# Gated linear attention and a GELU network: last output chunk by column halves, odd positions' sums by subtraction, another order

## The chip, the cores and the metric

The kernel runs on one core of a Trainium2 chip. The time is the device time of one execution in microseconds (us); of the kernel before there are 14 executions, with a median of 183.11 us (182.71 to 183.54). The core has a matrix engine (TensorE, PE in the profile, with its weight loads as PEld), VectorE (DVE), ScalarE (ACT) and GpSimd (POOL), and SyncE (SP), which issues most transfers. Matmul results lie in eight banks of PSUM.

## The reference

Attention with a decaying state, per batch (4) and head (8), over 768 positions with 48 numbers each:

```python
f = 1.0 / (1.0 + np.exp(-f_logit))
for t in range(S):
    state = f[:, :, t, :, None] * state + np.einsum('bhd,bhe->bhde', k[:, :, t], v[:, :, t])
    y[:, :, t] = np.einsum('bhd,bhde->bhe', q[:, :, t], state)
```

The result, as 3072 tokens of 384 numbers, goes through a network with 2048 hidden numbers:

```python
h = x @ w_in
g = 0.5 * h * (1.0 + erf(h * inv_sqrt2))
out = g @ w_out
```

## The kernel before

**Attention by chunks.** The 3072 tokens are 24 chunks of 128, six to a batch. Two chunks make a unit (12 units). Within a chunk the recurrence is made of products: with G the running sum of log f over the chunk, keys are scaled by exp(-G) and queries by exp(G); the masked scores of scaled queries and keys times v give the part from within the chunk; the scaled queries times the state before the chunk give the rest; and the state goes on by the keys times v and by the decay over the whole chunk. A batch's last chunk (5, 11, 17, 23) hands no state on.

**Units 0 to 4 are loaded in pairs** (`PAIRS`): each partition holds two neighbouring positions of a head, an even and an odd one, so that a transfer's pieces are twice as long. Rows 0 to 63 are then the unit's first chunk and rows 64 to 127 its second. The other units hold a chunk in their 128 rows.

**Steps and names.** An operation's name is a letter code with the number of its unit or chunk.

- `decays` (from L452): E and L (L479, L482) make -log f of a whole unit on ScalarE, in `lf`. C (L495 to L505) are TensorE's running sums, by multiplication with triangular matrices: in a pair unit two 128x384 matmuls for the even positions (C of the even number) and two for the odd ones, and eight narrow matmuls with `negp` (L505) for the decay over each of the two chunks; in other units one 128x384 matmul and four one-column ones with `negcol` (L497) per chunk. RG and GT (L510, L512) are exp(-G) and exp(G), GL (L515, L519) the decay over the chunk, all on ScalarE. KP and QP (L525) are the scaled keys and queries in `sc`, mostly on VectorE; VC (L530) casts v on GpSimd.
- `turn`: T (L558) transposes keys and queries on TensorE for units 0 to 3, KQ copies the result out; from unit 4 on a transposing transfer, KD (L546), does it.
- `attn_pair` and `attn_nat`: A are the scores (L724, L662), masked by VectorE (AM, L571); S the state product (L746, L685), `carry` its sum on VectorE (R, L591 and L595), decay (T, L597) and cast (SB, L602) on GpSimd; YI (L766) with YX (L645), or Y (L639, L698), the output, YB (L615) its copy. In a pair unit the matmuls use 64-row or 64-column tiles of the array; these operations have `mode=1`.
- X: the output is transposed for the network, by TensorE (L631) for units 0 to 4 and by a transposing transfer XD (L619) afterwards.
- `ffn_group`, one group per unit: eight F1 products (L802, six 128x256 matmuls each, hidden numbers by tokens), each followed by a GELU on ScalarE (GE, L812), then per chunk four F2 products (L821, four 128x384 matmuls each), added up in one bank; O (L836) copies the result, st (L841) stores it. For the last chunk, 23, the two halves of the columns are copied by ScalarE and VectorE (L829) and stored by two queues (L831).

**Banks.** `BANKS = (4, 0, 4)`: banks 0 to 3 (`s_fh`) are for F1 and F2 products and, at the start, for a few others; banks 4 to 7 (`s_m`) for the attention. An F1 product gives its bank back when its GELU has read it.

**Order.** The kernel issues nothing as it is written: `P.add` lists operations with an engine, an assumed duration, what they read and write, the buffers they use, and a priority; `Plan.run` places them one by one on its own clock, by the time at which they could start and then by priority, and so fixes each engine's order (each engine works through its order strictly). Priorities get a random part per range of 20 in the priority's number (`SEEDS`). ScalarE needs one table for exp and log and another for GELU; the planner groups these uses, and 15 loads (L870) stand between them, besides the first. `LOADS` is the order of the first loads: f, k, v, q of a unit (f2 is that of unit 2; u all four), i and o pieces of the two weight matrices, issued by GpSimd. In `load`, a transfer that follows one of the other queue is held until an earlier transfer of that queue has landed; for a load on SP this is the last but one of them.

**Filler.** At the end of the listing, before an operation that opens a bank and is planned before 30 us, matmuls of zeros are put in, as many as the planned idle time of TensorE holds (L864). They write the bank that the operation then uses.

Of the kernel before, what the change touches and what calls it, by code (L numbers as in the profile page):

```python
# [12 lines left out]
ALU = mybir.AluOpType  # L13
# [13 lines left out]

SEEDS = [0, 684, 383, 3363, 2427, 131, 74, 3619, 3555, 1021, 519, 3174]

# [52 lines left out]
class Plan:  # L82
# [30 lines left out]
    def run(self):  # L113
# [4 lines left out]
        for o in self.ops:  # L118
            if o.prio > -5:
                k = min(max(int(o.prio % 1000) // 20, 0), len(SEEDS) - 1)  # L120
                o.prio += rng.uniform(-SPREAD, SPREAD)
                if SEEDS[k]:
                    w = (0.5, 1.0, 3.0, 8.0)[SEEDS[k] % 4]
                    o.prio += own[k].uniform(-w, w)
        act, switched, mode = None, 0.0, 0
        port = {"DVE": (0.0, 0.0), "POOL": (0.0, 0.0)}
# [77 lines left out]


SIZES = [2, 2, 2, 2, 2, 2, 2, 2, 2, 2, 2, 2]
PAIRS = [0, 1, 2, 3, 4]
# [15 lines left out]
AJ = [2, 3, 4, 5, 6, 7, 8, 10, 11]  # L223
NGT = 4
ROWS = [16, 17, 18, 19]
WARM = 30.0
LOADS = ['f0', 'k0', 'v0', 'q0', 'f1', 'v1', 'k1', 'q1', 'i0', 'k2', 'f2', 'v2', 'q2', 'i1', 'i2', 'i3', 'o0', 'o1', 'o3', 'f3', 'o2', 'k3', 'q3', 'u4', 'v3']
LOADS += [f"u{n}" for n in range(12) if f"u{n}" not in LOADS and f"c{2 * n}" not in LOADS and f"f{n}" not in LOADS]
# [3 lines left out]
def kernel(  # L232
# [53 lines left out]
    s_gt, s_rg = slots(3, [C, HD], F32, "gt"), slots(3, [C, HD], F32, "rg")  # L286
    s_gl = slots(6, [C, 2, P2], F32, "gl")
    s_kq = slots(3, [C, 2, P2, 2, C], BF16, "kq")
    s_am = slots(8, [C, P2, C], BF16, "am")
# [52 lines left out]
    for i in range(3):  # L342
        P.add("DVE", 0.2, lambda i=i: nc.vector.memset(
            s_sb.tiles[i].rearrange("p a b -> p (a b)").bitcast(F32), 0.0), wr=[f"sbz{i}"], prio=-70)
    z_lf = [f"lfz{i}" for i in range(3)]
    z_sc = [f"scz{i}" for i in range(NQ)]
# [105 lines left out]
    def decays(u):  # L452
# [16 lines left out]
        for a, b, lo, hi in parts:  # L469
# [7 lines left out]
            def expop(lo=lo, hi=hi):  # L477
# [6 lines left out]
                  bufs=[fl, lf], table="exp", prio=pr, name=f"L{u}")  # L484
        gps = [(s_fh if u in EG else s_m).new() for _ in range(2)]
        for j, n in enumerate(ns):
            y = X[n]
            gt, rg = s_gt.new(), s_rg.new()
            y.update(sc=s_sc.new(), vb=s_vb.new())
            pr = 20 * u + 10 * j  # L490

            def cum(j=j, g=gps[j]):
                g = g.t()
                if not pair:
                    nc.tensor.matmul(g[:, 0:HD], trin, lf.t()[:, j, :, 0:D], start=True, stop=True)  # L495
                    for p in range(P2):
                        nc.tensor.matmul(g[:, HD + p:HD + p + 1], lf.t()[:, j, 2 * p:2 * p + 2, :], negcol,  # L497
                                         start=True, stop=True, skip_group_check=True)
                    return
                nc.tensor.matmul(g[:, 0:HD], trip[:, 0, :], lf.t()[:, 0, :, 0:D], start=True, stop=False)  # L500
                nc.tensor.matmul(g[:, 0:HD], trip[:, 1 - j, :], lf.t()[:, 1, :, 0:D], start=False, stop=True)
                if j:
                    for i in range(2):
                        for p in range(P2):
                            nc.tensor.matmul(g[:, HD + 2 * p:HD + 2 * p + 2], lf.t()[:, i, 2 * p:2 * p + 2, :], negp,  # L505
                                             start=False, stop=(i == 1), skip_group_check=True)
            P.add("PE", (0.54 if j else 0.33) if pair else 0.27, cum,
                  rd=([("lf", u, 0), ("lf", u, 1), "trip", "negp"] if pair else [("lf", u, j), "trin", "negcol"]), wr=[("g", n)],
                  bufs=[lf, gps[j], gt, rg, y["sc"], gl], prio=pr, opens=gps[j], name=f"C{n}")
            P.add("ACT", 0.40, lambda g=gps[j], rg=rg: nc.scalar.activation(rg.t(), g.t()[:, 0:HD], AF.Exp, scale=-1.0),  # L510
                  rd=[("g", n)], wr=[("rg", n)], bufs=[gps[j], rg], table="exp", prio=pr, name=f"RG{n}")
            P.add("ACT", 0.40, lambda g=gps[j], gt=gt: nc.scalar.activation(gt.t(), g.t()[:, 0:HD], AF.Exp),  # L512
                  rd=[("g", n)], wr=[("gt", n)], bufs=[gps[j], gt], table="exp", prio=pr + 1, name=f"GT{n}")
            if not pair:
                P.add("ACT", 0.19, lambda g=gps[j], j=j: nc.scalar.activation(  # L515
                    gl.t()[:, j, :], g.t()[:, HD:HD + P2], AF.Exp),
                    rd=[("g", n)], wr=[("gl", n)], bufs=[gl, gps[j]], table="exp", prio=pr + 2, name=f"GL{n}")
            elif j:
                P.add("ACT", 0.19, lambda g=gps[j]: nc.scalar.activation(  # L519
                    gl.t(), g.t()[:, HD:HD + 2 * P2].rearrange("a (p c) -> a c p", c=2), AF.Exp),  # L520
                    rd=[("g", n)], wr=[("gl", n - 1), ("gl", n)], bufs=[gl, gps[j]], table="exp", prio=pr + 2,
                    name=f"GL{n}")
            for w, nm, a, b, off in ((0, "kp", "kt", rg, 0), (1, "qp", "qt", gt, 1)):
                pl = n in (GKP, GQP)[w]
                P.add("POOL" if pl else "DVE", 0.80 if pl else 0.475, lambda w=w, a=a, b=b, y=y, j=j, pl=pl: (nc.gpsimd if pl else nc.vector).tensor_tensor(  # L525
                    y["sc"].t()[:, w, :, 0:D], half(u, x[a], j), b.t().rearrange("p (h d) -> p h d", h=H), ALU.mult),
                    rd=[("gt" if w else "rg", n), (a, n)] + z_sc, wr=[(nm, n)], bufs=[y["sc"], x[a], b], prio=pr + off,
                    port=True, name=f"{nm.upper()}{n}")
# [39 lines left out]
    def mask_scores(aps, ams, key, nm, rd, pr, mk, mkey):  # L568
        for hh in range(2):
            pl = key[1:] + (hh,) in GAM  # L570
            P.add("POOL" if pl else "DVE", 1.15 if pl else 0.61, lambda hh=hh, pl=pl: (nc.gpsimd if pl else nc.vector).tensor_tensor(  # L571
                ams[hh].t(), aps[hh].t().rearrange("p (h t) -> p h t", t=C),
                mk.unsqueeze(1).to_broadcast([C, P2, C]), ALU.mult),
                rd=[rd, mkey], wr=[key + (hh,)], bufs=[aps[hh], ams[hh]], prio=pr + PRI["A"], name=nm)
# [131 lines left out]
    def attn_pair(u):  # L706
# [52 lines left out]
        def intra():  # L759
            for hh in range(2):  # L760
                for p in range(P2):
                    h = 2 * p + hh
                    for jk in range(2):
                        for cc in range(2):
# [4 lines left out]
                                             skip_group_check=True)  # L769
        P.add("PE", 0.5, intra, mode=1, rd=[("am", u, a, b) for a in range(2) for b in range(2)] + [("vb", n) for n in ns],  # L770
              wr=[("yi", n) for n in ns] + ([("yp", n0)] if osb is None else []), bufs=yps + vbs + sum(ams, []) + [U[u]["yb"]],
              prio=pr + PRI["Y"], opens=yps[0], name=f"YI{u}")
        for cc, n in enumerate(ns):
            o = (osb, mid)[cc]
# [8 lines left out]
    def ffn_group(g):  # L783
# [11 lines left out]
        for u in range(FO // pk):  # L795
# [11 lines left out]
            def gelu(u=u, hps=hps):  # L807
                to, fr = gT.t()[:, u * pk:(u + 1) * pk, :].rearrange("p a b -> p (a b)"), hps.t()
                if U[ns[0] // 2]["pair"]:
# [4 lines left out]
                  name=f"GE{g}.{u}")  # L814
        for s_ in range(s):
            op, osb = s_fh.new(), s_os.new()
            n = first[g] + s_
            for r in range(4):
                def f2(s_=s_, r=r, op=op):
                    for fo in range(4 * r, 4 * r + 4):  # L820
                        nc.tensor.matmul(op.t()[:, 0:d_model], gT.t()[:, fo, s_ * C:(s_ + 1) * C], wout[fo // 4][:, fo % 4, :],  # L821
                                         start=(fo == 0), stop=(fo == FO - 1))
                P.add("PE", 0.65, f2, rd=[("gT", g, fo // pk) for fo in range(4 * r, 4 * r + 4)] + [f"wout{r}"],
                      wr=[("o", n)], bufs=[op, gT], prio=pr + PRI["F"] + s_, held=True, name=f"F2.{n}.{r}")
            if n == NCH - 1:
                osbs = (osb, s_os.new())
                for i, eng in enumerate(("ACT", "DVE")):
                    h = slice(i * d_model // 2, (i + 1) * d_model // 2)
                    P.add(eng, 0.27, lambda h=h, i=i, op=op, osb=osbs[i]: copier(not i)(osb.t()[:, h], op.t()[:, h]),  # L829
                          rd=[("o", n)], wr=[("os", n, i)], bufs=[op, osbs[i]], prio=pr - 1000, name=f"O{n}")  # L830
                    P.add("DMA", 0.3, lambda h=h, i=i, n=n, osb=osbs[i]: (nc.sync if i else nc.scalar).dma_start(  # L831
                        out=out[n * C:(n + 1) * C, h], in_=osb.t()[:, h]), rd=[("os", n, i)], bufs=[osbs[i]], prio=-5, lag=4.0,
                        name=f"st{n}")
                continue
            od = n in ODVE
            P.add("DVE" if od else "ACT", 0.475 if od else 0.40, lambda op=op, osb=osb, od=od: copier(not od)(osb.t(), op.t()[:, 0:d_model]),  # L836
                  rd=[("o", n)], wr=[("os", n)], bufs=[op, osb], prio=pr - 1000, name=f"O{n}")
            def store(n=n, osb=osb):
                w = C // 2 if n in ROWS else C
                for r in range(0, C, w):  # L840
                    nc.sync.dma_start(out=out[n * C + r:n * C + r + w, :], in_=osb.t()[r:r + w, :])  # L841
            P.add("DMA", 0.6, store, rd=[("os", n)], bufs=[osb], prio=-5, lag=4.0, name=f"st{n}")

    g = 0
# [59 lines left out]
```

## Time and profile before

| | |
|---|---|
| median of 14 executions | 183.11 us (182.71 to 183.54) |
| the profiled execution | 183.15 us |
| its span, from first to last instruction | 181.0 us |
| TensorE matmuls busy | 172.6 us (95%), 1991 instructions |
| ScalarE busy | 126.2 us (70%) |
| VectorE busy | 95.6 us (53%) |
| GpSimd busy | 52.5 us (29%) |
| F1 matmuls (L802) | 576, 273 ns each |
| F2 matmuls (L821) | 384, 326 ns each |
| GELU (L812) | 96, 667 ns each |
| table loads (L870) | 15, 1283 ns each |
| TensorE clock granted | full all through |

A row of the profile names line, engine and operation, then what is written and read, with its shape. A matmul's duration there includes the time until its last result is out, which overlaps with the next matmul; what a matmul costs in a dense run is the distance from its start to the next start. Where the order of time is shown, a bracket gives the engine's idle time before the instruction and what ended it. One execution has been profiled.

### The profile page before, as it was taken

Reading aid. Unit: us, or ns where it says so; the run is one execution under the profiler, and the core shown is the slowest. Engines: PE = TensorE matmul, PEld = TensorE weight load, DVE = VectorE, ACT = ScalarE, POOL = GpSimd, SP = SyncE. Lnnn points to the kernel's source line nnn. Section 1 sums busy time; section 2 is a strip of 40 time slices with the busy share of each in tenths; the row PEclk is TensorE's granted clock in tenths of the full one; section 3 lists DMA queues with packets and bytes.
Section 4 is the critical chain, followed back from the end, with each engine's and each line's share of the span. In section 5 each row is a group of like instructions: output and inputs, shape, how many; then the busy total and the mean of one; then the engine's idle time right before and its main releaser. Section 6 shows DMA issues by size and latency. Waiting matters only on the chain.

```text
span 181.0 us, 4913 instructions
## 1 busy us (share of the span) xinstructions
PE 172.6 (95%) x1991; PEld 131.8 (73%) x1991; DVE 95.6 (53%) x185; ACT 126.2 (70%) x215; POOL 52.5 (29%) x116
## 2 busy tenths in 40 slices
PE   7789989999999999999999999999999999999992
PEld 2356669865778977669679689966696976886961
DVE  4289730068898640689277771627785307171020
ACT  2775298992986899988957789687493698360910
POOL 7657870003224801251352014014353111100000
PEclk9999999999999999999999999999999999999999
DMA  5999999999989897999999979989999963812112
GB/s 143 267 261 224 272 187 210 216 259 270 274 154 234 164 213 140 221 187 213 176 201 229 179 153 231 179 172 160 193 249 120 222 118 74 175 48 43 43 43 87
DMA packets 106997, 32.61 MB, mean 180 GB/s; under 512 B 102112, under 2 KB 106080, under 8 KB 106976
## 3 DMA queue, kind: packets, MB, share of 16 engines
q1 hardware_dynamic: 105056, 29.07, 78.2%
q0 software_dynamic: 1776, 3.15, 9.7%
q8 instruction: 15, 0.25, 0.6%
q10 hardware_dynamic: 144, 0.10, 0.2%
q14 instruction: 6, 0.05, 0.1%
HBM read 25.17 MB, written 4.72 MB: 165 GB/s over the span
## 4 chain that ended last, share of the span: by engine, by line
PE 76%; DMA 8%; SPq 6%; ACT 4%; DVE 2%; issue 2%; DVEq 0%; ACTq 0%
PE ps L802 33%; PE ps L821 30%; SPq L434 6%; DMA fl<-in_f_logit_dram 6%; DMA xT<-yb 2%; PE ps L662 2%; PE ps L698 2%; ACT L870 1%; PE ps L495 1%; ACT gT L812 1%; PE ps L639 1%; DVE sc L525 1%; PE ps L685 1%; PE ps L724 1%; PE ps L558 1%
## 5 line engine op out<-in xcount | busy, mean ns | idle before, releaser
L812 ACT ACTIVATE gT<-ps 128x512 bf16<-128x512 f32 x96 | 58.4, 667 | 23.5 <-PE ps L802 21.9
L802 PE MATMUL ps<-xT,win 128*128 128x256 bf16 x576 | 68.6, 273 | 0.2 <-DMA xT<-yb 0.2
L821 PE MATMUL ps<-wout,gT 128*128 128x384 bf16 x384 | 68.3, 326 | 0.0
L802 PEld LDWEIGHTS <-win 128*128 128x128 bf16 x576 | 61.3, 114 | 2.6 <-issue 0.4
L821 PEld LDWEIGHTS <-gT 128*128 128x128 bf16 x384 | 35.9, 98 | 20.9
L525 DVE TENSOR_TENSOR sc<-kt,rg 128x384 bf16<-128x384 f32 x23 | 14.5, 632 | 29.1 <-ACT rg L510 28.2
L597 POOL TENSOR_TENSOR tn<-rr,gl 128x384 f32<-128x384 f32 x16 | 13.9, 868 | 40.8 <-DVE rr L595 35.8
L530 POOL CAST vb<-vt 128x384 bf16<-128x384 f32 x22 | 12.1, 560 | 44.9 <-DMA vt<-in_v_dram 44.8
L571 DVE TENSOR_TENSOR am<-ps,mask 128x512 bf16<-128x512 f32 x28 | 17.5, 684 | 12.3 <-PE ps L662 12.3
L836 DVE COPY osb<-ps 128x384 f32<-128x384 f32 x20 | 11.1, 555 | 23.7 <-PE ps L821 17.6
L870 ACT ACT_TABLE_LOAD x15 | 19.2, 1283 | 0.3
L602 POOL CAST sb<-tn 48x192 bf16<-48x192 f32 x40 | 14.5, 362 | 13.3 <-DVE tn L591 7.7
L615 DVE CAST yb<-ps 128x384 bf16<-128x384 f32 x22 | 12.0, 555 | 7.3 <-PE ps L698 4.1
L510 ACT ACTIVATE rg<-ps 128x384 f32<-128x384 f32 x24 | 12.0, 502 | 5.4 <-PE ps L497 4.6
L512 ACT ACTIVATE gt<-ps 128x384 f32<-128x384 f32 x24 | 11.8, 499 | 5.6 <-PE ps L505 3.7
L479 ACT ACTIVATE fl<-fl 128x768 f32<-128x768 f32 x12 | 10.2, 854 | 6.5 <-DMA fl<-in_f_logit_dram 6.4
L571 DVE TENSOR_TENSOR am<-ps,maskp 128x512 bf16<-128x512 f32 x20 | 12.5, 684 | 2.6 <-PE ps L724 2.5
L525 DVE TENSOR_TENSOR sc<-qt,gt 128x384 bf16<-128x384 f32 x23 | 13.0, 571 | 1.2 <-DMA kt<-in_k_dram 0.9
L864 PE MATMUL ps<-junk 128*128 128x512 bf16 (+2 forms) x35 | 10.1, 421 | 1.9 <-POOL junk L856 1.3
L482 ACT ACTIVATE lf<-fl 128x768 bf16<-128x768 f32 x12 | 10.1, 844 | 0.4
L595 DVE TENSOR_TENSOR rr<-ps,tn 128x384 f32<-128x384 f32 x16 | 8.8, 553 | 1.4 <-POOL tn L597 0.5
L864 PEld LDWEIGHTS <-junk 128*128 128x128 bf16 x35 | 3.5, 111 | 5.9 <-issue 3.2
(68 smaller groups left out, 125.3 us busy)
## 6 DMA issues: line engine op xcount, KB each, us to landing
out_dram<-osb SPq DMA_DIRECT2D x19, 192.0 KB, 2.3
fl<-in_f_logit_dram SPq DMA_DIRECT2D x14, 192.0 KB, 3.8
kt<-in_k_dram SPq DMA_DIRECT2D x14, 192.0 KB, 3.9
qt<-in_q_dram SPq DMA_DIRECT2D x14, 192.0 KB, 3.8
vt<-in_v_dram SPq DMA_DIRECT2D x14, 192.0 KB, 3.7
fl<-in_f_logit_dram SPq DMA_DIRECT2D x5, 384.0 KB, 5.6
kt<-in_k_dram SPq DMA_DIRECT2D x5, 384.0 KB, 5.9
vt<-in_v_dram SPq DMA_DIRECT2D x5, 384.0 KB, 6.7
```

What stands on the lines that cost most here:

```text
L510: P.add("ACT", 0.40, lambda g=gps[j], rg=rg: nc.scalar.activation(rg.t(), g.t()[:, 0:HD], AF.Exp, scale=-1.0), rd=[("g", n)], wr=[("rg", n ...
L525: P.add("POOL" if pl else "DVE", 0.80 if pl else 0.475, lambda w=w, a=a, b=b, y=y, j=j, pl=pl: (nc.gpsimd if pl else nc.vector).tensor_tensor(
L530: P.add("ACT" if hv else "POOL", 0.40 if hv else 0.47, lambda y=y, j=j, hv=hv: (nc.scalar.copy if hv else nc.gpsimd.tensor_copy)(y["vb"].t ...
L571: P.add("POOL" if pl else "DVE", 1.15 if pl else 0.61, lambda hh=hh, pl=pl: (nc.gpsimd if pl else nc.vector).tensor_tensor(ams[hh].t(), ap ...
L597: P.add("POOL", 0.83, lambda: nc.gpsimd.tensor_tensor(tn.t(), rr.t(), glb(), ALU.mult), rd=[("rr", n), ("gl", n)], wr=[("tn", n)], bufs=[r ...
L602: P.add("POOL", 0.36, lambda hh=hh: nc.gpsimd.tensor_copy(sb.t()[64 * hh:64 * hh + D, :, D * hh:D * hh + D], tn.t()[64 * hh:64 * hh + D, : ...
L615: P.add("ACT" if help_ else "DVE", 0.40 if help_ else 0.475, lambda: copier(help_)(yb.t()[:, i, :], yp.t()[:, 0:HD]), rd=[("yp", n)], wr=[ ...
L802: nc.tensor.matmul(hps.t()[:, i * tok:(i + 1) * tok].rearrange("a (s t) -> a s t", s=s), col(fo)[:, kk, :], xT.t()[:, :, kk, :], start=(kk ...
L812: nc.scalar.activation(to, fr, AF.Gelu)
L821: nc.tensor.matmul(op.t()[:, 0:d_model], gT.t()[:, fo, s_ * C:(s_ + 1) * C], wout[fo // 4][:, fo % 4, :], start=(fo == 0), stop=(fo == FO ...
L864: nc.tensor.matmul(o.opens.t()[:, 0:w], junk[:, 0:C], junk[:, 0:w], start=True, stop=True, skip_group_check=True)
L870: nc.scalar.preload_act_table_set({"exp": "natural_log_exp_and_others", "gelu": "gelu_and_others"}[o.table])
```

## The change

- **Column halves.** The second product (F2) of chunk 23 is made in two runs of 16 matmuls of 192 columns, for the first and the second half of the columns, each in a bank of its own. Each half is copied and stored as before, the first by ScalarE and its queue, the second by VectorE and SP.
- **Odd positions.** In units 2, 3 and 4 (`G1D`) the running sum at an odd position is the one at the even position before it less the odd position's own -log f: one VectorE subtraction (G), from PSUM and `lf` into a new SBUF tile, in place of two matmuls. The narrow matmuls for the chunk ends go to the even positions' operation.
- **No unused decay.** For the last chunk of a batch the narrow matmuls and the exponential of the decay are left out (in unit 2, the eight matmuls have one column instead of two). The decay tiles are set to 1 at the start by six memsets on VectorE.
- **Pair outputs.** In units 2, 3 and 4 (`YJ`) YI and YX are one operation.
- **Order.** Other `SEEDS`, and in `LOADS` the piece o2 stands before f3, not behind it. `NUDGE`, `XA`, `GLD` and `AMX` are empty or zero and change nothing.

```diff
-SEEDS = [0, 684, 383, 3363, 2427, 131, 74, 3619, 3555, 1021, 519, 3174]
+SEEDS = [1643, 41, 3215, 1275, 2533, 2502, 823, 887, 1264, 763, 2447, 3095]
...
-LOADS = [..., 'o1', 'o3', 'f3', 'o2', 'k3', 'q3', 'u4', 'v3']
+LOADS = [..., 'o1', 'o3', 'o2', 'f3', 'k3', 'q3', 'u4', 'v3']
...
+    for i in range(6):
+        P.add("DVE", 0.07, lambda i=i: nc.vector.memset(s_gl.tiles[i], 1.0), wr=[f"glz{i}"], prio=-60)
...
+        last = 2 * u + 1 if (2 * u + 1) % nC == nC - 1 else None
+            ends = 1 if last else 2
...
-                    for p in range(P2):
+                    for p in range(0 if gld or n == last else P2):
                         nc.tensor.matmul(g[:, HD + p:HD + p + 1], lf.t()[:, j, 2 * p:2 * p + 2, :], negcol,
...
+            if j and g1d:
+                P.add("DVE", 0.475, lambda a=gps[0], b=gps[1]: nc.vector.tensor_tensor(
+                    b.t().rearrange("p (h d) -> p h d", h=H), a.t()[:, 0:HD].rearrange("p (h d) -> p h d", h=H),
+                    lf.t()[:, 1, :, 0:D], ALU.subtract), ..., name=f"G{n}")
...
+        if u in YJ:
+            olds = [(cc, o) for cc, o in enumerate((osb, mid)) if o is not None]
+            def joint():
+                intra()
+                for cc, o in olds:
+                    interp(yps[cc], kq, cc, o)
+            P.add("PE", 0.5 + 0.2 * len(olds), joint, mode=1, ...)
...
+        for i, eng in enumerate(("ACT", "DVE") if first[g] + s == NCH else ()):
+            n, s_ = NCH - 1, s - 1
+            op, osb = s_fh.new(), s_os.new()
+            h = slice(i * d_model // 2, (i + 1) * d_model // 2)
+            w = d_model // 2
+            for r in range(4):
+                def f2(r=r, op=op, h=h, w=w):
+                    for fo in range(4 * r, 4 * r + 4):
+                        nc.tensor.matmul(op.t()[:, 0:w], gT.t()[:, fo, s_ * C:(s_ + 1) * C], wout[fo // 4][:, fo % 4, h], ...)
+            P.add(eng, 0.27, lambda ...: copier(not i)(osb.t()[:, 0:w], op.t()[:, 0:w]), ...)
+            P.add("DMA", 0.3, lambda ...: (nc.sync if i else nc.scalar).dma_start(
+                out=out[n * C:(n + 1) * C, h], in_=osb.t()[:, 0:w]), ...)
```

The order that the new program gives each engine differs from the old one nearly everywhere after the first units. Where it bears on the prediction: behind the first GELU the filler is four matmuls of 512 columns and one of 256, where it was three of 512. On TensorE, before the scores of unit 2 (A2) stand two more F2 products where one stood. In group 2 the order is four F1, A3, F1, F1, S3, F1, S4, F1, YI3, where it was F1, A3, three F1, S3, F1, YI3 with S4. In group 4 two F1, four F2, S10 and six F1 follow one another, where one F1 and twelve F2 products stood before the next F1 of that group. Behind the last output of the attention 28 F2 matmuls stand before the last group's F1 in both. On ScalarE the table loads are as many as before.

## The prediction

> **What bounds the kernel now.** I read the busy times and the chain that ended last, then busy time by stage, then the order of time around each stop of TensorE.
>
> ```profile
> PE 172.6 (95%) x1991; PEld 131.8 (73%) x1991; DVE 95.6 (53%) x185; ACT 126.2 (70%) x215; POOL 52.5 (29%) x116
> ...
> PE 76%; DMA 8%; SPq 6%; ACT 4%; DVE 2%; issue 2%; DVEq 0%; ACTq 0%
> ```
>
> TensorE works 95% of the span and is three quarters of the last chain. The rest of the chain is the start (SP, the load of fl) and the end. By stage (span; busy us and count of PE, PEld, DVE, ACT, POOL; clock, DMA share, GB/s):
>
> ```profile
> 26.00:34.70 8.70, 8.64 (x76) 8.25 (x76) 0.00 (x0) 8.23 (x15) 0.41 (x1) 1.00 1.12 205
> 34.70:52.00 17.30, 17.17 (x220) 11.48 (x218) 12.87 (x25) 12.66 (x26) 3.73 (x7) 1.00 1.11 253
> ...
> 68.00:80.00 12.00, 11.83 (x99) 8.03 (x98) 5.51 (x10) 11.15 (x23) 3.15 (x6) 1.00 0.94 169
> ...
> 135.00:141.00 6.00, 5.83 (x67) 4.61 (x63) 3.51 (x6) 2.34 (x6) 1.51 (x3) 1.00 1.01 144
> ```
>
> From 26 us to 177.7 us TensorE all but never stops, at full clock. So the time is: when that run starts, plus the matmul work in it, plus its few stops, plus the tail after its last matmul. The order of time (start, duration, engine, instruction, idle before) shows the start and the stops:
>
> ```profile
> 26.06 0.81 PE L864 MATMUL ps<-junk 128*128 128x512 bf16 x3 [0.62 <-ACT gT L812]
> 26.71 8.02 PE L802 MATMUL ps<-xT,win 128*128 128x256 bf16 x72
> 34.57 4.06 PE L821 MATMUL ps<-wout,gT 128*128 128x384 bf16 x24
> ...
> 40.56 0.81 PE L821 MATMUL ps<-wout,gT 128*128 128x384 bf16 x4
> 41.51 0.64 PE L724 MATMUL ps<-kq 64*64 64x128 bf16 x32
> ...
> 79.11 0.34 PE L685 MATMUL ps<-vb,sc 128*128 128x96 bf16 x4 [0.17 <-DVE sc L525]
> ...
> 91.75 0.34 PE L685 MATMUL ps<-vb,sc 128*128 128x96 bf16 x4 [0.20 <-DVE sc L525]
> ...
> 140.09 1.47 PE L802 MATMUL ps<-xT,win 128*128 128x256 bf16 x12 [0.17 <-DMA xT<-yb]
> ```
>
> Prices from start to start (a duration includes the pipeline's drain, which the next matmul covers): 24 F2 matmuls take 38.47 - 34.57 = 3.90, 0.1625 each; 72 F1 take 7.86, 0.109 each. By the same measure the four stops lost 0.30 (40.56 + 0.65 to 41.51), 0.33, 0.37 and 0.33 us: 1.33 in all. And three filler matmuls stand between the first gelu and the first F1 behind it: they wait for that gelu, since they write its bank, and cost 0.65 us of the path.
>
> **The change, part by part.**
>
> *Odd positions by VectorE, units 2 to 4.* Two 128x384 matmuls go from each unit; their price:
>
> ```profile
> 43.72 0.34 PE L505 MATMUL ps<-negp,lf 128*128 128x2 bf16 x8
> 43.92 0.32 PE L500 MATMUL ps<-lf,trip 128*128 128x384 bf16 x1
> ...
> 44.24 1.46 PE L821 MATMUL ps<-wout,gT 128*128 128x384 bf16 x8
> ```
>
> 44.24 - 43.92 = 0.32. Unit 2's pair stands before 25.3 us, where TensorE then waits for the gelu: worth nothing. Units 3 and 4 lie in the full run: -0.65. The three subtractions that VectorE gets are nearest to rr<-ps,tn (553 ns); unit 2's falls into VectorE's 12.5 us of idle before 37.5, the other two into stages where it is busy 12.9 of 17.3 us. The exponentials behind them are queued on ScalarE after other work, so I take nothing; without that cover each costs 0.7.
>
> *No end sum for a batch's last chunk.* Four one-column matmuls go at chunks 11, 17 and 23: 67.96 to 68.06 for such a four, so -0.30. Chunk 5 keeps its eight, one column narrower: nothing. Three 189 ns exponentials leave ScalarE.
>
> *Pair outputs in one run.* Each run of small-tile matmuls costs about 0.1 us when it begins (8 interpolation matmuls took 0.29, 16 in one run 0.47) and again when it ends (six F1 behind one took 0.77, not 0.66). Unit 2's second interpolation joins its run, but in the new order unit 4's state product leaves the run it stood in: 17 runs after 26 us in both orders. Nothing.
>
> *Column halves.* 16 matmuls of 384 columns (2.60) become 32 of 192. By these rows a matmul takes its columns / 2.4 GHz plus 2.5 ns, so 0.0825 x 32 = 2.64: +0.04. The Trainium skill ("TensorE: Matmul & The Clock Gate", Back-to-back issue gap) speaks against it: in a stream of weight loads and matmuls it gives 81 ns for 128 columns and 131 for 512; between them 192 would be an estimated 89 ns, 2.86 in all, +0.26. But eight 128-column transposes, each with its weight load, took 0.44 here (38.47 to 38.91), 55 ns each, and F2 takes 162 where the rule would give 114; I take +0.04.
>
> *Tail.*
>
> ```profile
> 177.74 0.32 ACT L829 COPY osb<-ps 128x192 f32<-128x192 f32 x1 [5.25 <-PE ps L821]
> ...
> 178.09 0.36 DVE L829 COPY osb<-ps 128x192 f32<-128x192 f32 x1 [2.34 <-ACT osb L829]
> 178.48 0.33 SPq L831 DMA_DIRECT2D out_dram<-osb  x1
> ```
>
> VectorE's half waits for ScalarE's, in the same bank. Now ScalarE's half is ready 1.3 us earlier, and VectorE starts at the last matmul's end: -0.35. Its store, 2.2 us to landing, stays last.
>
> *The start.* New order, same first gelu: ScalarE waits 3.59 us for the load of fl of unit 2, whose place among the loads is unchanged. This covers rg and gt being swapped in unit 0 (0.4 us) and six more memsets on VectorE, which idles 4.5 us there. But the filler behind the first gelu grows from 3 x 512 columns to 4.5 x 512, as one cumulative sum less leaves more planned room: 1.5 x 0.217 = +0.33 on the path.
>
> *Load order.* fl of unit 3 now follows wout 2. In the old order SP held it until wout 1 had landed (33.67) and the next load until wout 3 had (35.35); now it waits for wout 3: issued 1.7 us later, so landing near 40.5 instead of 38.65. Its two activations take 1.7, and the sum that needs them stands at about 44.2: 1.9 us to spare. k, q of unit 3 follow it on SP and keep their place. Two stores now stand before unit 4's and unit 3's v on SP and wait for output copies: unit 3's v goes out some 2.9 us later; its casts ended at 50.8, its product stands near 55.9: hidden, 2.2 to spare.
>
> *New priorities: the stops.* TensorE's four old stops: the first is filled by one more F2 before the score product. From the sum to the state product of chunk 12 there are now 2.45 us of matmuls (1.82 before); that of chunk 15 is moved behind three F1 products; and from the output of chunk 19 to the F1 that needs its transposing transfer there are 6.05 (4.74 before, where 5.07 were needed). I count all four as gone. Two new stops, both where four F1 or F2 products fill the four wide banks and the fifth must wait for a gelu behind a table load (1.28 us):
>
> - Group 2, after the scores of unit 3. From the start of unit 2's joint output: TensorE needs 0.97 + 0.55 + 0.52 + 0.34 + 0.65 + 0.22 + 0.65 + 0.655 + 0.22 + 1.97 + 0.57 = 7.32 to the fifth. ScalarE starts its copy at 1.17 and has 0.36 + 0.39 + 1.03 + 0.37 + 6 x 0.39 + 0.20 = 4.69 of copies and exponentials, then the load's 1.28, then gelu and release 0.82: 7.96. Stop 0.65.
> - Group 4, after one state product. From the last F1 of group 3: TensorE needs 0.655 x 2 + 2.60 + 0.17 + 0.655 = 4.74, then waits 0.2 for VectorE's output copy and runs one more, to 5.6. ScalarE: last gelu 0.9, load 1.28, five exponentials 1.75, load 1.28, gelu 0.75, release 0.1: 6.1. Stops 0.7.
>
> Bounds: 0 each if ScalarE runs ahead, 1.2 each if a copy or a VectorE product between is late. I add 0.25 for small new covers (the state product of chunk 13, the transfer of chunk 11). New stops 1.6 against 1.33: +0.27.
>
> **Sum** against the profiled execution (183.15 us, of which 181.0 are span): -0.65 - 0.30 + 0.04 + 0.33 + 0.27 - 0.35 = -0.66, so 182.49. It stands 0.04 above the median of 183.11, so 182.5 is the forecast.
>
> **Rivals.**
>
> *Slower: fl of unit 3 comes too late.* It must land by 42.4, 7.1 us after its issue at 35.3; the five such loads took 5.6 in the median and 10.3 at most, at a time when DMA is full. ScalarE runs in order, so every us beyond is a us for all its exponentials and for TensorE. From 8.1 us on the kernel is slower by over 0.37; at 9 us, 1.9 late, 184.4. Against it: before, it took 5.0 in the same crowd.
>
> *The work goes, the stops take it.* With both bank stops at their upper end and the small covers doubled, stops are 2.6 to 2.9: gain 0.1 or less, 183.1. For it: ScalarE is busy 11.15 of 12 us in that stage. Against it: the old order's planned covers failed by only 0.3 at a time.
>
> *The new order has no stops worth naming.* Stops 0.5: -1.76, 181.4 to 181.8. For it: ScalarE loses three exponentials, and from 92 to 135 us the old order had none.
>
> *The tail is not shortened*, as the store's landing is what counts: 182.85; inside the range.
>
> **How the numbers follow.** A measurement of this kernel tells about 0.2% (0.37 us) from no change. Forecast, with the tail case, 0.50, its own range 182.1 to 182.74; no stops 0.17; stops take it 0.15; late load, or anything that acts like it, 0.18. Faster 0.67, same 0.15, slower 0.18. The range goes from 181.6 (few stops) to 183.6, which leaves out the larger part of the late-load case and the best of the no-stop case, 2 in 10.
>
> **What would show it.** Right: first F1 after the first gelu about 1.0 us after that gelu's release instead of 0.65; no stop before the score product of unit 2; stops of 0.5 to 0.8 near 54 and 79 us, released by ScalarE's gelu; VectorE's last copy starting within 0.05 us of the last matmul, not of ScalarE's. Wrong: the halves taking over 2.75 us; ScalarE waiting over 2 us for fl of unit 3; stops of a us or more after 90 us, where I found none.

## The result, and the profile after

The changed kernel takes 182.12 us in the median (181.94 to 182.36, 10 runs) against 183.14 us (182.67 to 183.81, 48 runs): a ratio of 0.9945, 95% interval 0.9934 to 0.9956. That is 1.0 us less; the forecast was 182.5 us, within 181.6 to 183.6. The span of the profiled execution is 180.06 us, against 181.02 before: 0.96 less.

First the page of the changed kernel: busy times, and the engines of the chain that ended last.

```profile
PE 171.7 (95%) x1990; PEld 132.4 (74%) x1990; DVE 96.5 (54%) x194; ACT 125.3 (70%) x212; POOL 53.4 (30%) x116
...
PE 76%; ACT 10%; DMA 9%; SPq 2%; issue 1%; DVE 1%; DVEq 0%
```

TensorE is busy 0.9 us less, about what the span lost. In the chain ScalarE has gone from 4% to 10%: TensorE now waits for it at two places where it did not before. The stages show where (span; busy us and count of PE, PEld, DVE, ACT, POOL; clock, DMA share, GB/s):

```profile
34.70:52.00 17.30, 17.30 (x225) 12.03 (x224) 12.24 (x24) 12.81 (x25) 2.74 (x5) 1.00 0.98 232
68.00:80.00 12.00, 11.53 (x103) 9.77 (x101) 4.30 (x10) 11.91 (x20) 2.71 (x6) 1.00 0.99 209
135.00:141.00 6.00, 6.00 (x55) 4.76 (x55) 1.12 (x2) 2.94 (x6) 2.33 (x6) 1.00 0.99 199
```

Two stages in which TensorE had gaps have none now; between 68 and 80 us its gaps grew, and ScalarE there is busy 11.91 of 12. The order of time on TensorE (start, duration, engine, instruction, idle before and its releaser) shows the first F1, the stops and the last product:

```profile
26.21 1.13 PE L947 MATMUL ps<-junk 128*128 128x512 bf16 x5 [0.75 <-ACT gT L885]
27.18 8.02 PE L875 MATMUL ps<-xT,win 128*128 128x256 bf16 x72
...
53.65 0.64 PE L784 MATMUL ps<-kq 64*64 64x128 bf16 x32
54.74 1.47 PE L875 MATMUL ps<-xT,win 128*128 128x256 bf16 x12 [0.45 <-ACT gT L885]
...
76.78 1.65 PE L875 MATMUL ps<-xT,win 128*128 128x256 bf16 x12
78.89 2.78 PE L875 MATMUL ps<-xT,win 128*128 128x256 bf16 x24 [0.46 <-ACT gT L885]
...
174.24 2.80 PE L917 MATMUL ps<-wout,gT 128*128 128x192 bf16 x32
```

From the first filler to the first F1 behind it are 27.18 - 26.21 = 0.97 us (0.65 before). The two stops behind the table loads are there, both released by a gelu; the four old ones are not. The order of time of the other engines shows ScalarE ahead of the first stop, the wait for the load of unit 3's fl, and the end:

```profile
41.12 0.85 ACT L494 ACTIVATE fl<-fl 128x768 f32<-128x768 f32 x1 [1.91 <-DMA fl<-in_f_logit_dram]
...
51.57 0.58 ACT L543 ACTIVATE rg<-g 128x384 f32<-128x384 f32 x1
52.00 0.56 ACT L549 ACTIVATE gt<-g 128x384 f32<-128x384 f32 x1
52.41 0.22 ACT L570 ACTIVATE gl<-ps 128x8 f32<-128x8 f32 x1
52.65 1.28 ACT L953 ACT_TABLE_LOAD   x1
53.94 4.34 ACT L885 ACTIVATE gT<-ps 128x512 bf16<-128x512 f32 x7
...
175.76 0.32 ACT L921 COPY osb<-ps 128x192 f32<-128x192 f32 x1 [3.32 <-PE ps L917]
177.14 0.36 DVE L921 COPY osb<-ps 128x192 f32<-128x192 f32 x1 [2.08 <-PE ps L917]
177.52 0.33 SPq L923 DMA_DIRECT2D out_dram<-osb  x1
```

VectorE's last copy is now released by TensorE, not by ScalarE's copy. Between the last matmul's end (177.04) and the end of the span (180.06) lie 3.02 us; before it was 3.31.

With each matmul charged with the time to the next start, the two profiles differ like this: first gelu +0.15; filler +0.32; cumulative sums -0.65; end sums -0.23; matmuls of small tiles and the changes to and from them -0.29; halves +0.04; stops -0.01 (1.32 instead of 1.33); tail -0.30. The sum is -0.97, against -0.96 in the spans. This is one profile of each kernel.

### The profile page after: what moved, and what is told of

Its sections match the earlier page's. It is cut to its first block, busy times and chain, and to the rows that moved or that the text cites. A ratio compares the mean times of both kernels' runs of the same rounds, so it can differ in the third digit from the quotient of the medians.

```text
span 180.1 us, 4916 instructions
## 1 busy us (share of the span) xinstructions
PE 171.7 (95%) x1990; PEld 132.4 (74%) x1990; DVE 96.5 (54%) x194; ACT 125.3 (70%) x212; POOL 53.4 (30%) x116
## 4 chain that ended last, share of the span: by engine, by line
PE 76%; ACT 10%; DMA 9%; SPq 2%; issue 1%; DVE 1%; DVEq 0%
PE ps L896 31%; PE ps L875 31%; DMA win<-in_moe_w_in_dram 5%; ACT L953 4%; DMA fl<-in_f_logit_dram 3%; ACT gT L885 3%; PE ps L722 2%; SPq L449 2%; PE ps L758 2%; PE ps L917 1%; PE ps L521 1%; PE ps L699 1%; PE ps L826 1%; ACT gt L549 1%; PE ps L745 1%; ACT rg L543 1%
## 5 line engine op out<-in xcount | busy, mean ns | idle before, releaser
L885 ACT ACTIVATE gT<-ps 128x512 bf16<-128x512 f32 x96 | 57.5, 671 | 24.6 <-PE ps L875 23.0
L896 PE MATMUL ps<-wout,gT 128*128 128x384 bf16 x368 | 66.0, 326 | 0.0
L896 PEld LDWEIGHTS <-gT 128*128 128x128 bf16 x368 | 34.2, 98 | 19.5
L576 DVE TENSOR_TENSOR sc<-qt,gt 128x384 bf16<-128x384 f32 x23 | 13.7, 602 | 13.7 <-ACT gt L549 13.7
L543 ACT ACTIVATE rg<-ps 128x384 f32<-128x384 f32 x21 | 10.3, 502 | 5.4 <-PE ps L523 3.2
L947 PE MATMUL ps<-junk 128*128 128x512 bf16 (+3 forms) x36 | 10.8, 437 | 2.1 <-POOL junk L939 1.3
L549 ACT ACTIVATE gt<-ps 128x384 f32<-128x384 f32 x21 | 10.2, 503 | 2.6 <-PE ps L523 1.9
```

Source lines behind the costliest of these rows:

```text
L549: P.add("ACT", 0.40, lambda g=gps[j], gtv=gtv: nc.scalar.activation(gtv(), g.t()[:, 0:HD].rearrange("q (p h d) -> q p h d", h=2, d=D), AF. ...
L885: nc.scalar.activation(to, fr, AF.Gelu)
L947: nc.tensor.matmul(o.opens.t()[:, 0:w], junk[:, 0:C], junk[:, 0:w], start=True, stop=True, skip_group_check=True)
```

## The experiments

Three sets of runs, each on a chip of its own, beside runs of the kernel before (183.04, 183.10 and 183.26 us in the median of the sets). Ratios are to those; differences between sets are safer by the ratios than by the times. My theory: TensorE's unbroken run sets the time, so matmul work and filler count in full; the two new stops are set by ScalarE's chain of exponentials and table load. Rivals: work taken from TensorE goes into stops; the stops wait for something else; the end is set by the landing of the store.

For reading the profiles, this table has three times of each: start of the first F1 behind the first gelu, end of the last matmul, and the stops of over 0.2 us between (us lost from start to start, at which time). The 0.65 at 54 us holds about 0.13 for the change of tile shape, the 0.30 at 41 us about 0.09.

| Kernel profiled | first F1 | last end | between | stops |
|---|---|---|---|---|
| before | 26.71 | 177.71 | 151.00 | 0.30 at 41, 0.33 at 79, 0.37 at 91, 0.33 at 140 |
| before, halves alone | 26.88 | 177.86 | 150.99 | 0.30 at 41, 0.33 at 79, 0.57 at 139 |
| before, joined run | 26.77 | 177.47 | 150.70 | 0.30 at 41, 0.32 at 79, 0.44 at 139 |
| before, no filler | 26.09 | 176.67 | 150.58 | 0.30 at 40, 0.32 at 78 |
| before, two exponentials twice | 26.67 | 177.58 | 150.91 | 0.30 at 41, 0.29 at 77, 0.39 at 79 |
| changed | 27.18 | 177.04 | 149.86 | 0.65 at 54, 0.18 + 0.62 at 78 |
| changed, again | 27.07 | 177.40 | 150.33 | the same two, 0.22 at 83, 0.31 at 131 |
| changed, no filler | 26.04 | 176.33 | 150.29 | the same two, 0.33 at 82 |
| changed, two exponentials twice | 27.15 | 178.09 | 150.94 | 1.19 at 54, 0.61 + 0.73 at 78 to 79 |
| changed, unit 2's sum twice | 27.31 | 177.46 | 150.15 | the same two, 0.31 at 92 |
| changed, units 3 and 4 twice | 27.53 | 178.76 | 151.23 | 0.35 at 55, 0.62 at 79, 0.82 at 93, 0.21 at 143 |
| changed, unit 3's sum twice | 27.08 | 177.98 | 150.90 | the same two, 0.24 at 83, 0.25 at 92, 0.37 at 131 |
| changed, unit 4's sum twice | 27.33 | 178.95 | 151.62 | 0.35 at 54, 0.62 at 78, 0.35 at 83, 0.35 at 92, 1.13 at 129 |
| changed, old end | 27.27 | 178.48 | 151.21 | 0.48 at 55, 0.62 at 79, 0.81 + 0.69 at 84 |

**The halves alone.** The kernel before, its last chunk's second product computed as in the change:

```diff
-            op, osb = s_fh.new(), s_os.new()
+            if n == NCH - 1:
+                break
+            op, osb = s_fh.new(), s_os.new()
...
+        for i, eng in enumerate(("ACT", "DVE") if first[g] + s == NCH else ()):
+            n, s_ = NCH - 1, s - 1
+            op, osb = s_fh.new(), s_os.new()
...
+                        nc.tensor.matmul(op.t()[:, 0:w], gT.t()[:, fo, s_ * C:(s_ + 1) * C], wout[fo // 4][:, fo % 4, h],
```

> The kernel before with the column halves of the last chunk alone, in two banks; every other instruction stands where it stood. Theory (tail as predicted: VectorE's copy no longer waits for ScalarE's): 0.04 more for the halves, 0.35 less for the tail, so 182.8 against 183.14, ratio 0.9983. Rival (the landing of the last store is what counts, or the halves cost what the page's rule says): 183.1 to 183.2.

Measured 182.88 us, ratio 0.9987 (0.9978 to 0.9997), -0.05 to -0.40 us: a gain; its middle is smaller than the -0.31 of my two terms, which the interval takes in. Order of time at its end:

```profile
175.06 2.80 PE L844 MATMUL ps<-wout,gT 128*128 128x192 bf16 x32
176.58 0.32 ACT L848 COPY osb<-ps 128x192 f32<-128x192 f32 x1 [3.97 <-PE ps L844]
177.95 0.36 DVE L848 COPY osb<-ps 128x192 f32<-128x192 f32 x1 [2.08 <-PE ps L844]
178.34 0.33 SPq L850 DMA_DIRECT2D out_dram<-osb  x1
```

VectorE starts 0.09 behind the last matmul's end (177.86); before, 178.09 - 177.71 = 0.38. So the mechanism holds and is worth 0.29 less 0.04. The rival that the store's landing alone sets the end falls.

**One run of small tiles more joined.** The kernel before, the interpolation of chunk 5 put right behind that of chunk 4:

```diff
+    at = {o.name: i for i, o in enumerate(P.placed) if o.name in ("YX4", "YX5")}
+    P.placed.insert(at["YX4"] + 1, P.placed.pop(at["YX5"]))
```

> The kernel before with unit 2's second interpolation moved up, directly behind the first, so that the three small-tile pieces of this output are one run; nothing else moves. Theory formed from the two traces (each change of the tile shape, also inside a run, costs about 0.1 us of TensorE): two changes less, 0.2 us faster, 182.9. Rival (the prediction's count by runs, with what it gained given back at the next stop): 183.1.

Measured 183.04 us, ratio 0.9999 (0.9987 to 1.0012). In its profile the stretch from the start of the joint output to the next F2 (46.14, 46.43, 46.76, 47.05 and 47.29 before) is

```profile
45.70 0.57 PE L766 MATMUL ps<-vb,am 64*128 64x48 bf16 x32
46.20 0.53 PE L645 MATMUL ps<-sb,kq 128*64 128x96 bf16 x16
46.66 0.62 PE L558 MATMUL ps<-ident,sc 128*128 128x128 bf16 x8
47.22 0.34 PE L631 MATMUL ps<-ident,yb 128*128 128x128 bf16 x3
47.40 0.81 PE L821 MATMUL ps<-wout,gT 128*128 128x384 bf16 x4
```

1.70 us instead of 1.81 (45.64 to 47.45). Two changes of shape are gone, and 0.11 us is won on the spot, not 0.2: the interpolations take 0.46 where the two parts took 0.29 each, but the eight transposes behind them take 0.56 (46.66 to 47.22) where eight took 0.44 elsewhere. In the time nothing of it is seen, within 0.24 us; whether it is given back at a later stop or is lost in the scatter stays open.

**No filler behind the first gelu**, in both kernels:

```diff
-WARM = 30.0
+WARM = 26.0
```

> The changed kernel without the filler matmuls behind the first gelu; no other instruction moves. Theory (the filler stands on TensorE's path): the first F1 behind the gelu starts 0.97 us earlier, and all of it reaches the end unless the weights' landing or the load of fl of unit 3 stops TensorE first: 181.2, at worst 181.5. Rival (the stage is paced by ScalarE's gelus and by loads, the filler fills time that is lost anyway): 182.0 to 182.2.

> The kernel before without its three filler matmuls behind the first gelu (filler planned up to 26 us instead of 30; nothing else moves). The gap from the gelu's release to the first F1 was 0.65 us; if the filler is on the path as in the changed kernel, 183.1 - 0.65 = 182.4 us. Rival: the next waits (xT by its transfer, win by its load) are as late, and nothing is won: 183.1 us. Set beside the changed kernel without filler (181.36), it gives what the change is worth with filler out of the way: my sum without the filler term says -0.99 (182.49 - 0.33 - 183.15), so 182.4 - 181.36 = 1.0 to 1.1.

The changed kernel without it takes 181.36 us, ratio 0.9901 (0.9887 to 0.9916); the kernel before without it 182.13 us, ratio 0.9945 (0.9927 to 0.9964). Order of time on TensorE, first of the changed kernel without filler, then of the kernel before without it:

```profile
26.04 8.02 PE L875 MATMUL ps<-xT,win 128*128 128x256 bf16 x72 [0.47 <-ACT gT L885]
```

```profile
26.09 8.02 PE L802 MATMUL ps<-xT,win 128*128 128x256 bf16 x72 [0.16 <-ACT gT L812]
```

The first F1 now starts right behind the gelu, where the filler did (26.04 and 26.09, against 27.18 and 26.71): the filler is on the path, and nothing else was waiting there. The granted clock stayed at full (1.00 from 26 us on in both profiles), so here the filler was not needed for it either. Of the changed kernel's 0.97 the median shows 0.76: its profile has a new stop of 0.33 before a transposed tile at 82 us. The rest of the gain of the kernel before (its median fell by 0.97, the start by 0.62) is, by its one profile, two stops that it lacks, at 91 and 140 us. With the filler out of both, the change is worth 182.13 - 181.36 = 0.77 us across two sets (0.81 by the ratios); the sum without its filler term had said 0.99. The changed kernel without filler is the fastest measured.

**Work put back on TensorE.** The changed kernel, the one cumulative sum of some units made twice (the second overwrites the first):

```diff
-                nc.tensor.matmul(g[:, 0:HD], trip[:, 0, :], lf.t()[:, 0, :, 0:D], start=True, stop=False)
-                nc.tensor.matmul(g[:, 0:HD], trip[:, 1 - j, :], lf.t()[:, 1, :, 0:D], start=False, stop=True)
+                for _ in range(2 if u in (3, 4) else 1):
+                    nc.tensor.matmul(g[:, 0:HD], trip[:, 0, :], lf.t()[:, 0, :, 0:D], start=True, stop=False)
+                    nc.tensor.matmul(g[:, 0:HD], trip[:, 1 - j, :], lf.t()[:, 1, :, 0:D], start=False, stop=True)
```

Units 3 and 4, then unit 2, unit 3 and unit 4 alone, and the changed kernel once more as their yardstick:

> The changed kernel with the two 128x384 sums of the even positions of units 3 and 4 made twice, into the same place, at the same point of TensorE's order: TensorE gets back in both units just the matmul time that the subtraction took from it. Theory (TensorE's work counts in full after 26 us): 0.65 more, 182.75. Rival (the subtraction's worth is hidden behind the two stops for a gelu, which then simply shrink): 182.1 to 182.3, since the stop behind unit 3's scores can swallow the second at most in part.

> The changed kernel with the two 128x384 matmuls of unit 2's one cumulative sum made twice (+0.33 us of TensorE before 26 us). My step: what TensorE does there is worth nothing, since it then waits for the first gelu: 182.1 us, within 0.1. Rival: ScalarE's exponentials behind the sum, and with them the gelu, move by the 0.33: 182.45 us.

> The changed kernel itself once more, as the yardstick for the three runs beside it and for a second profile: 182.1 us; the two bank stops at 54 and 78 us (0.65 and 0.62 from start to start) again, as they are set by ScalarE's fixed chain; a stop near 92 us before the F1 that needs chunk 11's transposing transfer may or may not be there (it was in two of five profiles of this order, 0.31 and 0.82 us, and in none of the other three).

> The changed kernel with the two matmuls of unit 3's one cumulative sum (44.3 us) made twice, +0.33 us of TensorE. ScalarE stands idle there until this sum is ready (2.18 us before its first exponential), so its chain moves with it, the stop at 54 us stays at 0.65, and the time grows by the whole 0.33: 182.45 us. Rival: half of it or less is seen, as ScalarE catches up before 54 us: 182.1 to 182.25 us.

> The changed kernel with the two matmuls of unit 4's one cumulative sum (48.3 us) made twice, +0.33 us of TensorE. ScalarE is busy without a gap from 48 us to the table load, and its exponentials of this sum stand at 50.5, two us behind it. So I expect ScalarE's chain where it was, the stop at 54 us smaller by 0.3 (0.65 to 0.35), and the time as it was: 182.1 to 182.2 us. Rival, the step of my prediction taken alone (each sum counts 0.33 wherever it lies in the full run): 182.45 us.

| Kernel | us, lowest to highest | ratio to before in its set |
|---|---|---|
| units 3 and 4 twice (first set) | 182.84 (182.46 to 183.67) | 0.9990 (0.9981 to 1.0000) |
| unit 2 twice (second set) | 182.43 (181.98 to 183.72) | 0.9973 (0.9950 to 0.9996) |
| changed, again (third set) | 182.66 (181.82 to 183.54) | 0.9975 (0.9951 to 0.9999) |
| unit 3 twice (third set) | 183.12 (182.44 to 184.39) | 1.0000 (0.9973 to 1.0026) |
| unit 4 twice (third set) | 183.60 (182.67 to 184.54) | 1.0014 (0.9990 to 1.0039) |

Both sums together cost 0.72 us over 182.12 (0.82 by the ratios), about the 0.65 of matmuls. But the profile (taken in the slowest of its 22 runs) doesn't show it as plain addition: the stop at 55 us is 0.30 smaller, and a stop of 0.82 has come at 93. Apart, unit 3's stands 0.46 over its yardstick, which is not clear of the scatter (the two intervals overlap), and its stop at 54 us is unchanged, as expected. Of unit 4's I had expected nothing. The stop at 54 us did shrink, from an idle of 0.45 to one of 0.15, but the time rose by 0.94 (here the intervals only just overlap). The order of time on TensorE says where it went:

```profile
54.10 0.64 PE L785 MATMUL ps<-kq 64*64 64x128 bf16 x32
54.89 1.47 PE L876 MATMUL ps<-xT,win 128*128 128x256 bf16 x12 [0.15 <-ACT gT L886]
...
92.97 0.70 PE L876 MATMUL ps<-xT,win 128*128 128x256 bf16 x5 [0.18 <-DMA xT<-yb]
...
130.27 0.40 PE L723 MATMUL ps<-kq 64*128 64x128 bf16 x8 [0.99 <-DMA kq<-sc]
```

Stops at 83, 92 and 129 us, all before a matmul that needs a tile from a transposing transfer. They are not a matter of unit 4's sum alone: the changed kernel itself, in this set, has two of that kind (0.22 and 0.31). It reaches a lower best time than in the first comparison (181.82) and a higher median. The transfer that ended the stop of 1.13 took 5.1 us to land; the slowest in the same window took 4.1 in the changed kernel's first profile. But the kernel before scatters in this set as widely (182.44 to 184.27, against 182.67 to 183.81 in the first comparison), so the scatter is not the new order's alone. So this part answers how the stop at 54 us behaves (what unit 4's sum adds ahead of it, it gives back), and leaves open why the time rose: the scatter is too large. The same goes for unit 2's: its run between first F1 and last end was 0.29 longer, and that is a stop of 0.31 at 92 us. Its first gelu was 0.13 us later, no more than runs of one kernel differ there (26.02 to 26.23 in five profiles of the order before), so that its extra matmuls were hidden is likely and not shown.

The tile view of the transposing transfers of kq that feed the products at 83 us, of the changed kernel in its first profile and then in its second (transfers with their issue, then time to landing):

```profile
L599 SPq DMA_TRANSPOSE kq<-sc x2: 1232/1283/1334, 76.7 to 78.6; - x2
DMA to landing us min/median/max: 3.2/3.8/4.4
```

```profile
L599 SPq DMA_TRANSPOSE kq<-sc x2: 1231/1257/1283, 76.6 to 78.4; - x2
...
  PEld L722: 0.2, 1
...
DMA to landing us min/median/max: 3.5/4.1/4.7
```

Issued at the same time, landing 0.3 later: nothing waits in the first, TensorE's weight load waits 0.2 in the second. At this place the new order leaves the transfers less than 0.3 us of slack.

**ScalarE made longer.** The exponential rg of chunks 9 and 11, ahead of the two gelu table loads at 52.65 and 76.80 us, made twice in the changed kernel, and the exponentials of the same chunks in the kernel before:

```diff
-            P.add("ACT", 0.40, lambda g=gps[j], rg=rg: nc.scalar.activation(rg.t(), g.t()[:, 0:HD], AF.Exp, scale=-1.0),
+            P.add("ACT", 0.40, lambda g=gps[j], rg=rg, n=n: [nc.scalar.activation(rg.t(), g.t()[:, 0:HD], AF.Exp, scale=-1.0) for _ in range(2 if n in (9, 11) else 1)],
```

> The changed kernel; ScalarE makes the exponential rg of chunks 9 and 11 twice (a repeated instruction just ahead of each of the two gelu table loads that end near 54 and 78 us; nothing else moves on any engine). The second one costs ScalarE about 0.37 to 0.39 us, by the starts of the exponentials in a row there. My reading: both stops of TensorE are set by ScalarE's chain (exponentials, table load, gelu, free bank), so each grows by that: stop 0.52 to about 0.9 at 54 us, 0.80 to about 1.2 at 78 us, time 182.12 + 0.75 = 182.85 us. Rival: the banks wait for something else (VectorE's copy or TensorE's own order) and ScalarE has room: 182.1 to 182.3 us.

> The kernel before with the same two exponentials made twice. There TensorE has no stop behind these table loads (it found four wide banks free for long enough), so I expect nothing of the first and little of the second: 183.0 to 183.3 us. Rival: ScalarE's chain sets TensorE's pace in the old order as well, then +0.75: 183.85 us. With the run of the same edit in the changed kernel it tells whether the new order leaves TensorE closer to ScalarE than the old one.

The changed kernel: 183.11 us, ratio 1.0003 (0.9990 to 1.0015), so the whole gain is gone. The order of time of ScalarE, then of TensorE:

```profile
51.54 1.14 ACT L543 ACTIVATE rg<-g 128x384 f32<-128x384 f32 x2
52.58 0.51 ACT L549 ACTIVATE gt<-g 128x384 f32<-128x384 f32 x1
52.99 0.16 ACT L570 ACTIVATE gl<-ps 128x8 f32<-128x8 f32 x1
53.17 1.28 ACT L953 ACT_TABLE_LOAD   x1
```

```profile
55.25 1.47 PE L875 MATMUL ps<-xT,win 128*128 128x256 bf16 x12 [1.00 <-ACT gT L885]
...
78.56 0.82 PE L875 MATMUL ps<-xT,win 128*128 128x256 bf16 x6 [0.44 <-DVE osb L901]
79.94 1.25 PE L875 MATMUL ps<-xT,win 128*128 128x256 bf16 x10 [0.57 <-ACT gT L885]
```

The pair takes 52.58 - 51.54 = 1.04 us instead of 0.43: the repeat cost 0.61 (0.56 at the other place), not the 0.37 I had put. The stops grew by 1.19 - 0.65 = 0.54 and by 1.34 - 0.80 = 0.54, together 1.08, and the run between first F1 and last end by just that. Both stops are ScalarE's. (The wait of 0.44 ends with a copy on VectorE, but that copy stands behind a product for which VectorE waited 0.33 us for the lengthened exponential.) In the kernel before the same edit gives 183.39 us, ratio 1.0006 (0.9990 to 1.0023): at most 0.42 us, against about 1.06 (0.0058 of 183.1) in the changed one. The new order stands on ScalarE's chain at two places where the old one did not.

**The old end in the changed kernel.** The last chunk's second product as 16 matmuls of 384 columns again, with two copies from one bank:

```diff
+            if n == NCH - 1:
+                osbs = (osb, s_os.new())
+                for i, eng in enumerate(("ACT", "DVE")):
...
-        for i, eng in enumerate(("ACT", "DVE") if first[g] + s == NCH else ()):
```

> The changed kernel with the old end: the last chunk's second product as 16 matmuls of 384 columns in one bank, and its two halves copied by ScalarE and VectorE from that bank; nothing ahead of it moves. My prediction's terms undone: +0.35 - 0.04 = 182.43 us. By the two profiles (last matmul's end to the end of the span 3.31 us against 3.06, halves 0.04 more): 182.33 us. Rival (the last store's landing counts, not the copy): 182.1 us.

Measured 182.77 us, ratio 0.9970 (0.9946 to 0.9994), 0.11 over its yardstick. It doesn't tell what it was made for: in this order the product of the chunk before the last came out last, with a copy of all 384 columns behind it:

```profile
178.52 0.56 DVE L909 COPY osb<-ps 128x384 f32<-128x384 f32 x1 [1.89 <-PE ps L894]
```

That is a third kind of end, not the old one, and what I wrote of nothing moving ahead of it was wrong. Its profile, near the slowest of its runs, also has the longest loss before transposed tiles at one place, 1.5 us at 84 us. There VectorE made the keys and queries within 0.1 us of when it did in the changed kernel's first profile, but their transfers went out 1.6 us later (78.3, not 76.7): SP, which works in order, was behind since a load of k that held it for 2.80 us, where it had taken 0.99. The size of the tail term rests on the two profiles and on the halves alone.

## Why the prediction was right, step by step

The prediction stood 0.4 us above the median. The path was right: when TensorE's run starts, its work, its stops and the tail. Most terms came out near their size; that the total did is in part luck, since misses of about 0.6 us to the fast side met 0.3 to the slow side.

- **Odd positions' sums, -0.65.** TensorE's cumulative sums fell by 0.65, and doubling the two that are left costs 0.72. No exponential behind the two subtractions waited for them in the profile, as forecast. The step took the sums as plain subtraction, with the stop reckoned apart, and together that holds. By itself unit 4's half only makes the stop at 54 us longer: with its work put back, 0.30 of the 0.65 is gone. The share of each unit in the time is not settled.
- **No end sum, -0.30.** -0.23: the price of four, taken from start to start, held a part that the matmul behind it pays anyway.
- **Pair outputs, nothing.** -0.29 with all small tiles. The count was right: 17 runs, and 37 changes of tile shape, in both profiles; what unit 2's joined output saves (1.43 us from 46.88 to 48.31, where the same matmuls took 1.65 from 45.64 to 47.29), the two changes of shape around unit 4's state product cost again, at about 0.1 each. What the step missed is a small stop inside the old run. Before, in order of time (S3, the F1 behind it, S4, the interpolation behind it):

```profile
54.93 0.51 PE L746 MATMUL ps<-vb,sc 64*128 64x96 bf16 x16
55.38 0.84 PE L802 MATMUL ps<-xT,win 128*128 128x256 bf16 x6
...
56.57 0.68 PE L746 MATMUL ps<-vb,sc 64*128 64x96 bf16 x16
57.18 0.36 PE L645 MATMUL ps<-sb,kq 128*64 128x96 bf16 x8
```

  S4's 16 matmuls took 0.61 where S3's took 0.45. The second of them, which in the program waits for VectorE, starts at 56.75, when VectorE's sum rr (L595, 56.14 to 56.70) is done. That is 0.16; the other 0.13 lies in smaller pieces and is not explained.
- **Halves, +0.04.** 2.64 us for 32, as worked out. The 2.86 us estimated from the figures of the Trainium skill ("TensorE: Matmul & The Clock Gate", Back-to-back issue gap) did not appear.
- **Filler, +0.33.** 0.97 instead of 0.65 us, +0.32. Taking it out moved the first F1 to the place of the filler in both kernels.
- **Stops, +0.27.** The two bank stops came where they were put: 0.52 without the change of shape (0.65 forecast) and 0.80 (0.7), set by ScalarE as the doubled exponentials show. The four old ones are gone. The 0.25 for small covers was the step that failed: it was 0 in the first profile, which makes the stops +0.0 instead of +0.27. It is not nothing in general. In other profiles of this order, most with small edits, 0.3 to 1.8 us in all is lost before transposed tiles at 82 to 84, 92 and 129 to 131 us. I had named one of the three places, chunk 11's transfer at 92.
- **Tail, -0.35.** -0.30: VectorE starts 0.1 behind the last matmul, not with it, and before it had started 0.38 behind.
- **Start.** The first gelu came 0.15 later, within what profiles of one kernel differ.
- **Load order.** The load of fl went out at 36.95, not 35.3, and ScalarE waited 1.91 us for it. This was nearer to the slower rival than I had put: I gave 1.9 us to spare; the logarithm ended at 42.83, and its sum stood at 44.31, so 1.5 were left. Hidden, as forecast, at this landing time of 4.1 us.

With the end sums at -0.23, the small tiles at -0.29, the filler at +0.32, the stops at -0.01 and the tail at -0.30 the same sum reads -1.12 instead of -0.66; the first gelu, 0.15 later, makes it -0.97. The rival of no stops worth naming (181.4 to 181.8) ends 0.3 us below the result, no further off than the forecast, but its mechanism is not what happened: stops of 1.32 us are there. The rival of the stops taking all was summed wrongly: with the other terms at -0.93, stops of 2.6 to 2.9 us instead of 1.33 give a loss of 0.3 to 0.6, so 183.5 to 183.8 us and not 183.1.

Against the forecast stands the third set: there the same two kernels differ by 0.0025 (0.0001 to 0.0049), not by 0.0055. The two intervals overlap a little. The extra transfer stops in the profile of that set point to a slack that the new order has lost. The wider scatter of both kernels on that chip is a rival; the two were not tried apart. So the gain was 1.0 us in the first comparison and about half of that in the third set.

## What to carry to other kernels

When one engine runs without a break, add up what changes in its own run from start to start, and then look at what it meets at the old times: a wait that goes (four here) tends to come back at the next engine in line (ScalarE's table load, and transfers with no slack). A stop has an owner, and lengthening the owner's chain by a known amount shows who it is: both stops grew by nearly what ScalarE's chain grew. Warm-up work that is planned by an estimate of idle time is to be checked against the trace; here 1 us of it stood behind the wait that it was to fill, and leaving it out was worth about 0.8 us, nearly as much as the whole change.

## What the runs showed of the hardware that I had not expected

- A second ScalarE exponential of 128x384 into the same tile starts later than one into another tile: it added 0.61 and 0.56 us, where exponentials in a row into different tiles start 0.37 to 0.43 apart.
- Changing the tile shape on TensorE costs about 0.1 us each time, inside a run of small tiles too: eight interpolation matmuls with the change behind them took 0.29, sixteen in one piece 0.46. Joining the two pieces saved 0.11 of the stretch.
- A transposing transfer of kq issued at the same time landed after 4.4 us at most in one run and 4.7 in another, 5.1 and 5.4 in runs of kernels with small edits. The changed kernel's runs lie within 0.42 us in the first comparison and within 1.72 in the third set; how much of that comes from these transfers is not shown, as the runs of the kernel before lie within 1.83 us in the third set too.
